# Longformer attention and a softplus MLP in one kernel: queries and keys of the first two batches loaded four tokens to a partition, and the written order of the work made anew

## The chip, the cores and the metric

The kernel runs on one core of a Trainium2 chip. The metric is the device time of one execution in microseconds, the median over the runs; lower is better. The core has a matrix engine (PE, with weight loads PEld), a vector engine (DVE), an activation engine (ACT), a general engine (POOL) and a sync engine (SP) that here only issues transfers. All five run their own written list of instructions in order and wait for one another through semaphores.

## What is computed

Attention over 8 batches, 8 heads, 576 tokens and 64 columns a head: a token sees its neighbours within 32 places, and 8 global tokens see and are seen by all. The result, 4,608 tokens of 512 columns, goes through a two-layer MLP with softplus between.

```python
def _attn_ref(q, k, v, global_idx):
    ...
    scores = scale * np.matmul(q, k.transpose(0, 1, 3, 2))
    mask = np.abs(pos[:, None] - pos[None, :]) <= window      # 32
    mask = mask | is_global[:, None] | is_global[None, :]
    scores = np.where(mask, scores, -1000000000.0)
    scores = scores - np.max(scores, axis=-1, keepdims=True)
    attn = np.exp(scores)
    attn = attn / (np.sum(attn, axis=-1, keepdims=True) + 1e-09)
    return np.matmul(attn, v)

def _moe_ref(x, w_in, w_out):                                 # 512 to 2048 to 512
    h = x @ w_in
    g = np.maximum(h, 0.0) + np.log1p(np.exp(-np.abs(h)))
    return g @ w_out
```

Inputs and output are float32; the products run in bfloat16 with float32 sums.

## The kernel before

**Tiling.** The sequence of a batch is cut into 18 blocks of 32 tokens. Four blocks of all 8 heads make a *pair* (36 pairs over 8 batches, `add_pair`); for a pair, scores of a block against its four key slots (previous, own, next, and one with the global keys) go through mask, maximum `m`, exponential `st`, sum `sm`, reciprocal `rs`, normalisation `pn`, and a 32 by 32 transpose to `pt`. Four pairs make a *phase* of 512 tokens (nine phases). The value products `xo` (L1210) take `pt`, and their result, copied to `xT`, is the input of the MLP: `h` (L1245) with `w_in`, softplus to `g` on ACT (L1251), and `o` (L1256) with `w_out`. The first phase is cut in three pieces (one, two and one pair), the second in two, so that the MLP can start early. Per batch the rows of the global tokens are computed beside that: scores `sg`, maxima `gm`, exponentials `pg`, transposes `pgt`, products `ov`, then `odd`, `both` and `vg`, which the value products need.

**The way in.** Batches 0 and 1 (`b < EARLY`) come in a way of their own: `load_part` loads a part of the sequence of all heads, with `e` neighbouring tokens on one partition, `cast` makes bfloat16 of one `e` of it, `tr` turns it on PE by four transposes and picks the global tokens by four small products (`hot`), and `trev` copies the turned tile from PSUM to `qx` or `kx`, with a stride of `e`. Before, two tokens lie on a partition: a part has 256 tokens, so there are two whole parts and a tail of 64 tokens for q and for k. `FIRST` is the order of the parts. Batches 2 to 7 are loaded by `load_qk` in strips of 32 columns and turned on DVE.

**Queues.** SP issues the loads of q, k and v, in the order of the plan; POOL issues the weights (`w_in` and `w_out`, four pieces each, cast to bfloat16 by the transfer) and most stores. Two things tie the queues together. `follow` lets SP load a few bytes out of `w_in[1]` (or `w_out[1]`), which makes SP wait for that piece before it issues what stands behind (L729). And POOL copies one element of a loaded tile to `seen` before it issues the first weights: of v's first half ahead of `w_in` (L1324), and of a part of batch 1's q ahead of `w_out` (L1388). A load on SP's queue also waits, eight loads later, for the semaphore that it shares with an earlier one.

**The order.** `_Order` is a planner inside the kernel. Every piece of work is a job with costs per engine and dependencies. `ORDER` is a list written out, 1,700 entries and some, that names each next job and its engine (`x // 5`, `x % 5`); a job's planned time `at` sorts them, and each engine's instructions are emitted in that order. So every engine's sequence is fixed by `ORDER`. The planner's costs have an effect on the built program in one place: `keep` puts filler products (`warm`, L706, which compute nothing that is used) on PE where it plans an idle stretch of over 700 ns before 34 us. `stall` models how PE's own instructions are fetched: in blocks of `BLOCK` = 256, the first block asked for at instruction `ASK` = 130 and needed at `NEED` = 442, each taking what `SLOW` says for that time. `settle` shares the transfers between SP's and POOL's queue, `SHARE` = 0.12 for SP when both have work. `SUMMED` names the pairs of the first phase whose sums DVE makes; for the others ACT's exponential adds up as it goes (L1079).

Of the kernel before, what the change touches and what calls it, by code (L numbers as in the profile page):

```python
# [19 lines left out]
class _Order:  # L20
# [20 lines left out]
    SLOW = ((29000, 7000), (37000, 4400), (51000, 6000), (62000, 4200), (150000, 4500), (1e9, 3900))  # L41
# [137 lines left out]
    def run(self, free):  # L179
# [9 lines left out]
        order = []  # L189
# [83 lines left out]
        order.sort(key=lambda j: (j["at"], j["n"]))  # L273
# [9 lines left out]
def kernel(  # L283
# [47 lines left out]
    SUMMED = (2,3,)  # L331
# [169 lines left out]
    for w, t in FIRST[0]:  # L501
        load_part(0, w, t)
# [926 lines left out]
```

## Time and profile before

| | us |
|---|---|
| median of 3 runs | 343.15 |
| lowest and highest | 342.66, 345.87 |
| the profiled execution | 343.51 |
| its span in the trace | 341.8 |
| PE busy | 316.4 |
| DVE busy | 251.3 |
| ACT busy | 221.1 |
| POOL busy | 184.4 |

The span is what the trace records from the first instruction to the last; the time has 1.71 us more around it. Busy time counts an engine's instructions but not its waits. Matmuls are pipelined, so PE's busy time is not its time at full rate, and about one in a hundred of its records is missing, which shows as gaps of 0.16 us. A line with an idle time in brackets says how long the engine had nothing to do just before, and what ended that.

### The profile page before, as it was taken

How to read it: one execution, taken by the hardware profiler on the slowest of the kernel's cores; microseconds unless marked ns; L12 is line 12 of the kernel's file. 1: busy time of each engine (PE TensorE's matmuls, PEld its weight loads, DVE VectorE, ACT ScalarE, POOL GpSimd, SP SyncE). 2: the span in 40 equal slices, each digit the busy share in tenths (PEclk: the TensorE clock that was granted, in tenths of full speed). 3: DMA queues.
4: the chain of work that ended last, by engine and by line, in shares of the span. 5: the costliest groups of instructions: out<-in, count | busy, mean ns of one | idle time of the engine just before them, and what ended most of it. 6: DMA issues, size and time to landing. Idle time of an engine off the chain costs nothing.

```text
span 341.8 us, 12136 instructions
## 1 busy us (share of the span) xinstructions
PE 316.4 (93%) x5278; PEld 171.6 (50%) x5323; DVE 251.3 (74%) x420; ACT 221.1 (65%) x436; POOL 184.4 (54%) x161
## 2 busy tenths in 40 slices
PE   6858889989999999999999999999799989999996
PEld 2725776466555444544554445444344444445453
DVE  7597588987998898999986488979676869631000
ACT  3696768946678868279637775576275747944342
POOL 6474718976696487939548467695415523210000
PEclk9567899999999999999999999999899999999999
DMA  7999399998999899970989798312100111011003
GB/s 192 232 197 256 73 177 169 164 150 169 202 185 175 141 208 199 209 135 31 181 128 181 151 188 224 74 25 46 65 33 11 54 66 63 0 61 63 2 0 123
DMA packets 168733, 42.74 MB, mean 125 GB/s; under 512 B 153192, under 2 KB 165736, under 8 KB 168680
## 3 DMA queue, kind: packets, MB, share of 16 engines
q1 hardware_dynamic: 160664, 28.33, 46.3%
q0 software_dynamic: 6144, 10.49, 13.0%
q10 hardware_dynamic: 1872, 3.15, 2.4%
q8 instruction: 41, 0.67, 0.8%
q14 instruction: 12, 0.10, 0.1%
HBM read 36.71 MB, written 9.44 MB: 135 GB/s over the span
## 4 chain that ended last, share of the span: by engine, by line
PE 66%; DVE 13%; SPq 5%; DMA 5%; issue 4%; ACT 3%; POOL 2%; ACTq 1%; DVEq 0%; POOLq 0%
PE h L1245 28%; PE o L1256 26%; PE xo L1210 4%; SPq L440 3%; PE s L1043 3%; DMA wout<-in_moe_w_out_dram 2%; DVE sm L1090 2%; DMA stage<-in_k_dram 2%; DVE m L1060 2%; SPq L445 2%; DVE st L1047 1%; DVE pt L1107 1%; DVE gm L945 1%; PE ov L968 1%; PE pick L852 1%
## 5 line engine op out<-in xcount | busy, mean ns | idle before, releaser
L1245 PE MATMUL h<-xT,win 128*128 128x512 bf16 (+3 forms) x756 | 136.6, 329 | 1.6 <-DVE xT L698 0.6
L1256 PE MATMUL o<-wout,g 128*128 128x512 bf16 (+1 forms) x561 | 130.9, 375 | 3.8 <-issue 3.2
L1251 ACT ACTIVATE g<-h 128x512 bf16<-128x512 f32 (+3 forms) x192 | 85.4, 496 | 47.9 <-PE h L1245 47.2
L1245 PEld LDWEIGHTS <-win 128*128 128x128 bf16 x768 | 67.3, 99 | 59.6 <-issue 1.3
L1256 PEld LDWEIGHTS <-g 128*128 128x128 bf16 x592 | 55.8, 98 | 63.5 <-issue 2.4
L1098 POOL TENSOR_TENSOR pn<-st,rs 128x1024 bf16<-128x1024 f32 (+1 forms) x36 | 62.4, 1737 | 43.0 <-DVE rs L1092 38.4
L1066 POOL TENSOR_TENSOR st<-st,m 128x1024 f32<-128x1024 f32 x27 | 54.1, 2014 | 48.1 <-DVE m L1060 48.0
L1047 DVE TENSOR_TENSOR st<-s,mask 128x512 f32<-128x512 f32 x64 | 41.3, 678 | 7.1 <-PE s L1043 7.0
L1090 DVE TENSOR_REDUCE sm<-st 128x8 f32<-128x1024 f32 (+1 forms) x36 | 41.1, 1141 | 4.4 <-ACT st L1083 3.8
L1060 DVE TENSOR_REDUCE m<-st 128x8 f32<-128x1024 f32 x32 | 38.1, 1210 | 0.4
L1083 ACT ACTIVATE st<-st 128x1024 f32<-128x1024 f32 x32 | 32.8, 1056 | 1.7 <-POOL st L1066 1.2
L1107 DVE STREAM_TRANSPOSE pt<-pn 128x512 int32<-128x512 int32 x36 | 24.6, 690 | 5.0 <-POOL pn L1098 5.0
L698 ACT COPY osb<-o 128x512 f32<-128x512 f32 (+1 forms) x25 | 14.2, 571 | 18.9 <-PE o L1256 11.8
L698 DVE CAST xT<-xo 128x512 bf16<-128x512 f32 (+3 forms) x25 | 13.1, 567 | 17.4 <-PE xo L1210 17.4
L698 ACT CAST xT<-xo 128x512 bf16<-128x512 f32 (+2 forms) x23 | 9.8, 475 | 19.1 <-PE xo L1210 19.1
L945 DVE TENSOR_REDUCE gm<-sg 128x1 f32<-128x320 f32 (+1 forms) x32 | 12.3, 445 | 9.1 <-PE sg L935 9.1
L1210 PE MATMUL xo<-pt,vb 32*64 32x96 bf16 (+2 forms) x1328 | 14.4, 212 | 4.3 <-issue 4.3
L698 POOL CAST kb<-stage 128x1152 bf16<-128x1152 f32 (+1 forms) x10 | 14.2, 1437 | 7.5 <-DVE st L1047 7.5
L1043 PE MATMUL s<-kx,qx 64*32 64x128 bf16 x1152 | 15.9, 229 | 1.5 <-ACT kx L698 0.7
L1043 PEld LDWEIGHTS <-qx 64*32 64x32 bf16 x1152 | 10.7, 94 | 12.6 <-issue 10.2
L698 POOL CAST vb<-stage 128x1152 bf16<-128x1152 f32 x13 | 15.7, 1223 | 1.6 <-DMA stage<-in_v_dram 1.6
L1210 PEld LDWEIGHTS <-vb 32*64 32x64 bf16 x1328 | 13.8, 104 | 4.9 <-issue 4.6
(125 smaller groups left out, 307.6 us busy)
## 6 DMA issues: line engine op xcount, KB each, us to landing
stage<-in_v_dram SPq DMA_DIRECT2D x64, 144.0 KB, 4.1
stage<-in_k_dram SPq DMA_DIRECT2D x48, 144.0 KB, 3.9
stage<-in_q_dram SPq DMA_DIRECT2D x48, 144.0 KB, 3.9
out_dram<-osb POOLq DMA_DIRECT2D x24, 256.0 KB, 3.4
out_dram<-osb ACTq DMA_DIRECT2D x11, 256.0 KB, 2.0
stage<-in_q_dram SPq DMA_DIRECT2D x4, 512.0 KB, 5.5
stage<-in_k_dram SPq DMA_DIRECT2D x4, 512.0 KB, 8.5
win<-in_moe_w_in_dram POOLq DMA_DIRECT2D x4, 512.0 KB, 7.6
```

Of the source, the lines that this page charges most:

```text
L698: {"ACT": nc.scalar.copy, "DVE": V.tensor_copy, "POOL": nc.gpsimd.tensor_copy}[e](out, in_)
L1043: nc.tensor.matmul(out=PS["s", n, g][quad(a ^ g), x, :], lhsT=qx[b % 2][rows(g), a, j * BL:(j + 1) * BL], rhs=kx[b % 2][rows(g), a, e0 * B ...
L1047: V.tensor_tensor(out=PS["st", n][:, h, :, :], in0=PS["s", n, h][:, :, :], in1=mask[:, h, j0:j0 + PB, :, :].rearrange("p j s i -> p j (s i ...
L1060: V.reduce_max(out=m[:], in_=flat(PS["st", n], h0, h1), axis=AX)
L1066: on(e).tensor_tensor(out=t, in0=t, in1=over(PS["m", n, y][:], SL * BL), op=OP.subtract)
L1083: nc.scalar.activation(out=t, in_=t, func=AF.Exp)
L1090: V.reduce_sum(out=sm[:], in_=flat(PS["st", n], h0, h1), axis=AX)
L1098: on(e).tensor_tensor(out=PS["pn", n][:, :, :, h0:h1].rearrange("p x s h -> p h x s"), in0=PS["st", n][:, h0:h1], in1=PS["rs", n, y][:].re ...
L1210: nc.tensor.matmul(out=PS["xo", v_, hd // 2][hd % 2 * D:(hd % 2 + 1) * D, (x - X0) * BL:(z - X0) * BL], lhsT=lhs, rhs=rhs, start=start, st ...
L1245: nc.tensor.matmul(out=h[:, :], lhsT=w_in_t[c // 4][:, kd, c % 4 * P:(c % 4 + 1) * P], rhs=PS["xT", m][:, kd, lo:hi], start=(kd == 0), sto ...
L1251: nc.scalar.activation(out=PS["g", m, c][:, lo:hi], in_=PS[key][:, lo_of(c, hi - lo)], func=AF.Softplus)
L1256: nc.tensor.matmul(out=PS["o", m, ns, a][:, :], lhsT=PS["g", m, kf][:, ns * P:(ns + 1) * P], rhs=w_out_t[kf // 4][:, kf % 4, a:z], start=( ...
```

## The change

Five things change.

1. For batches 0 and 1 four tokens lie on a partition (`EP = 4`): a part has 512 tokens (1 MB of float32), so there is one whole part and the tail of 64. The casts, transposes and evictions keep their number and sizes; only strides change. The load of q and k of a batch takes 2 transfers of 1 MB, in runs of 1 KB, in place of 4 of 512 KB in runs of 512 B.
2. `FIRST`: k's part comes first, then q's, then the tails. The loads of batch 0 are issued by their jobs, so they too stand where the plan has them: k, q, k's tail, half of v, q's tail, the other half of v.
3. The copy to `seen` ahead of `w_out` reads batch 1's one whole q part, the first of that batch's loads, in place of its second, the last.
4. The planner's numbers: `SLOW` (longer fetches), the lengths of the early loads, the costs of the masked exponentials; `SUMMED` is empty, so ACT adds up in all four pairs of the first phase. Jobs of equal planned time keep the order in which they were planned.
5. `ORDER` is a new list. Every engine's sequence is new: among other things SP issues batch 1's q part ahead of the wait for `w_in[1]`, and the first half of batch 1's v ahead of the wait for `w_out[1]`; the first stretch of `h` has 60 products (48 before) and takes `w_in[3]` after eight of them; two of the eight normalisations of the first phase run on DVE; there are 42 fillers in place of 19, 17 of them at the start, 2, 11, 8 and 4 further on; and the two score blocks of the first two pairs follow each other.

```diff
-    SLOW = ((29000, 7000), (37000, 4400), (51000, 6000), (62000, 4200), (150000, 4500), (1e9, 3900))
+    SLOW = ((30000, 9300), (37000, 6500), (51000, 7300), (62000, 6500), (250000, 5600), (1e9, 4200))
...
-        order.sort(key=lambda j: (j["at"], j["n"]))
+        order.sort(key=lambda j: j["at"])
...
-    SUMMED = (2,3,)
+    SUMMED = ()
...
     ORDER = (
...
-    NTOK = 2 * P
+    EP = 4
+    NTOK = EP * P
     FULL = S // NTOK
-    PARTS = [(t, e) for t in range(FULL) for e in range(2)] + [(FULL, 0)]
+    PARTS = [(t, e) for t in range(FULL) for e in range(EP)] + [(FULL, 0)]
...
-            nc.sync.dma_start(out=flat(stage[w])[:, t * 2 * HD:(t + 1) * 2 * HD].rearrange("p (h x) -> p h x", h=H),
-                              in_=SRC[w][b, :, t * NTOK:(t + 1) * NTOK, :].rearrange("h (p e) d -> p h (e d)", e=2))
+            nc.sync.dma_start(out=flat(stage[w])[:, t * EP * HD:(t + 1) * EP * HD].rearrange("p (h x) -> p h x", h=H),
+                              in_=SRC[w][b, :, t * NTOK:(t + 1) * NTOK, :].rearrange("h (p e) d -> p h (e d)", e=EP))
...
-    FIRST = ([(0, 0), (1, 0), (1, 1), (1, 2), (0, 2), (0, 1)], [(0, 0), (1, 0), (1, 1), (1, 2), (0, 2), (0, 1)])
-    assert FULL == 2
+    FIRST = ([(1, 0), (1, 1), (0, 0), (0, 1)], [(1, 0), (0, 0), (1, 1), (0, 1)])
+    assert FULL == 1
...
-    for w, t in FIRST[0]:
-        load_part(0, w, t)
...
-                if b:
-                    load_part(b, w, t)
+                load_part(b, w, t)
...
-                                       moves=(2000 if b else 1750) if t < FULL else 1500 if b else 600)
+                                       moves=(3500 if b else 3000) if t < FULL else 1300 if b else 650)
...
-                copy(eng, keys[:, :, 4 * t:4 * t + 4, e:2 * BL:2], ps.rearrange("p a (c i) -> p a c i", i=BL))
+                copy(eng, keys[:, :, n * t:n * t + n, e:2 * BL:EP], ps.rearrange("p a (c i) -> p a c i", i=D // EP))
             else:
-                copy(eng, qx[i][:, :, t * NTOK + e:(t + 1) * NTOK:2], ps)
+                copy(eng, qx[i][:, :, t * NTOK + e:(t + 1) * NTOK:EP], ps)
...
-            T["ex", n, y] = o.add({"ACT": act(k, False) if not masked else (720, 820) if n in SUMMED else (1480, 1580)}, lambda e, y=y: ex(e, y), [job, *gate],
+            T["ex", n, y] = o.add({"ACT": act(k, False) if not masked else (1050, 1150) if n in SUMMED else (1390, 1490)}, lambda e, y=y: ex(e, y), [job, *gate],
...
-            T["landed"] = o.add(pool(100), lambda e: nc.gpsimd.tensor_copy(seen[:, 0, :], natural(0, 1)[:, 0, 0, 0, 0:1]), [T["part", 1, 0, FULL]], rank=0)
+            T["landed"] = o.add(pool(100), lambda e: nc.gpsimd.tensor_copy(seen[:, 0, :], natural(0, 0)[:, 0, 0, 0, 0:1]), [T["part", 1, 0, 0]], rank=0)
```

More of the change, by code (lines that the diff above doesn't have):

```diff
@@ L478, in natural @@
         if t < FULL:
-            return x[:, t * 2 * HD:(t + 1) * 2 * HD].rearrange("p (g a e d) -> p g a e d", g=2, a=HG, e=2)
-        return x[:, 2 * FULL * HD:2 * FULL * HD + HD // 2]
+            return x[:, t * EP * HD:(t + 1) * EP * HD].rearrange("p (g a e d) -> p g a e d", g=2, a=HG, e=EP)
+        return x[:, EP * FULL * HD:EP * FULL * HD + HD // 2]
     def rounded(w, t, e):
@@ L484, in rounded @@
         if t < FULL:
-            return x[:, (2 * t + e) * HD:(2 * t + e + 1) * HD]
-        return x[:, 2 * FULL * HD:2 * FULL * HD + HD // 2]
+            return x[:, (EP * t + e) * HD:(EP * t + e + 1) * HD]
+        return x[:, EP * FULL * HD:EP * FULL * HD + HD // 2]
     def load_part(b, w, t):
         if t < FULL:
-            nc.sync.dma_start(out=flat(stage[w])[:, t * 2 * HD:(t + 1) * 2 * HD].rearrange("p (h x) -> p h x", h=H),
-                              in_=SRC[w][b, :, t * NTOK:(t + 1) * NTOK, :].rearrange("h (p e) d -> p h (e d)", e=2))
+            nc.sync.dma_start(out=flat(stage[w])[:, t * EP * HD:(t + 1) * EP * HD].rearrange("p (h x) -> p h x", h=H),
+                              in_=SRC[w][b, :, t * NTOK:(t + 1) * NTOK, :].rearrange("h (p e) d -> p h (e d)", e=EP))
             return
@@ L518 @@
     count(pp[:], [[0, 1]], 0, 1)
-    count(pt_[:, 0:2 * FULL], [[NTOK, FULL], [1, 2]], 0, 2)
+    count(pt_[:, 0:EP * FULL], [[NTOK, FULL], [1, EP]], 0, EP)
     for g in range(2):
-        count(pt_[rows(g), 2 * FULL:], [[0, 1]], FULL * NTOK, 1)
+        count(pt_[rows(g), EP * FULL:], [[0, 1]], FULL * NTOK, 1)
     count(pos[:, P:], [[1, S - P]], P, 0)
@@ L811, in tr @@
         def tr(w, t, e):
-            if e == 0:
-                PS["tr", b, w, t] = psum(("tr", b, w, t), [P, 2, HG, P], BF16)
-            ps = PS["tr", b, w, t]
+            if e % 2 == 0:
+                PS["tr", b, w, t, e // 2] = psum(("tr", b, w, t, e // 2), [P, 2, HG, P], BF16)
+            ps = PS["tr", b, w, t, e // 2]
             own = (qkey, kkey)[w]
@@ L818, in tr @@
             x = rounded(w, t, e)
-            z = 2 * t + e
-            done = [u for v_, u in FIRST[b] if v_ == w][-1] == t and (e or t == FULL)
+            z = EP * t + e
+            done = [u for v_, u in FIRST[b] if v_ == w][-1] == t and (e == EP - 1 or t == FULL)
             for a in range(HG):
                 if t < FULL:
-                    nc.tensor.transpose(out=ps[:, e, a, :], in_=x[:, a * P:(a + 1) * P], identity=ident[:, :])
+                    nc.tensor.transpose(out=ps[:, e % 2, a, :], in_=x[:, a * P:(a + 1) * P], identity=ident[:, :])
                 else:
                     for g in range(2):
-                        nc.tensor.transpose(out=ps[rows(g), e, a, 0:D], in_=x[rows(g), a * D:(a + 1) * D], identity=ident[rows(g), rows(g)])
+                        nc.tensor.transpose(out=ps[rows(g), e % 2, a, 0:D], in_=x[rows(g), a * D:(a + 1) * D], identity=ident[rows(g), rows(g)])
             for a in range(HG):
@@ L836, in trev @@
         def trev(eng, w, t, e):
-            ps = PS["tr", b, w, t][:, e]
+            ps = PS["tr", b, w, t, e // 2][:, e % 2]
+            n = NTOK // D
             keys = near_keys(0, 2 * BL)
             if t == FULL:
-                copy(eng, keys[:, :, 4 * t, :] if w else qx[i][:, :, t * NTOK:], ps[:, :, 0:D])
+                copy(eng, keys[:, :, n * t, :] if w else qx[i][:, :, t * NTOK:], ps[:, :, 0:D])
             elif w:
-                copy(eng, keys[:, :, 4 * t:4 * t + 4, e:2 * BL:2], ps.rearrange("p a (c i) -> p a c i", i=BL))
+                copy(eng, keys[:, :, n * t:n * t + n, e:2 * BL:EP], ps.rearrange("p a (c i) -> p a c i", i=D // EP))
             else:
-                copy(eng, qx[i][:, :, t * NTOK + e:(t + 1) * NTOK:2], ps)
+                copy(eng, qx[i][:, :, t * NTOK + e:(t + 1) * NTOK:EP], ps)
         def pck(e, ws):
@@ L883, in add_prep @@
             for w, t in FIRST[b]:
-                for e in range(2 if t < FULL else 1):
+                for e in range(EP if t < FULL else 1):
                     n = HD if t < FULL else HD // 2
@@ L889, in add_prep @@
                     last = T["last", w]
-                    k_ = ("tr", b, w, t)
+                    k_ = ("tr", b, w, t, e // 2)
                     T["last", w] = T["tr", b, w, t, e] = o.add({"PE": (330, 500) if b else (640, 810) if t == 0 else (500, 670)}, lambda eng, w=w, t=t, e=e: tr(w, t, e),
                                          [job, last, *had("make_ident", "make_hot")], rank=3 if b else 1, ins=16 if t < FULL else 32, array=128 if t < FULL else 64,
-                                         opens=([("tr", k_)] if e == 0 else []) + ([("pick", ("pick", b, w))] if t == e == 0 else []),
-                                         uses=([k_] if e else []) + ([("pick", b, w)] if t + e else []))
+                                         opens=([("tr", k_)] if e % 2 == 0 else []) + ([("pick", ("pick", b, w))] if t == e == 0 else []),
+                                         uses=([k_] if e % 2 else []) + ([("pick", b, w)] if t + e else []))
                     T["cast", b, w].append(job)
```

144 rows, old and new, of the table ORDER are left out of this document.

## The prediction

> **What bounds the kernel now.** I read the page first: busy shares, then the 40 slices.
>
> ```profile
> PE 316.4 (93%) x5278; PEld 171.6 (50%) x5323; DVE 251.3 (74%) x420; ACT 221.1 (65%) x436; POOL 184.4 (54%) x161
> PE   6858889989999999999999999999799989999996
> PEclk9567899999999999999999999999899999999999
> ```
>
> PE is the bound, but for four slices at the front, a dent near slice 28 and the end; its clock is down at the front and in that same dent. PE's products do not change in number, so the time can only change where PE idles or runs at a low clock. The view by stretches shows where (from:to, length, PE busy and, in the first row, the other engines; the last three numbers are clock, DMA share, GB/s).
>
> ```profile
> 36.00:40.00 4.00, 4.00 (x30) 3.05 (x27) 2.81 (x8) 2.18 (x12) 2.37 (x8) 0.57 0.14 38
> 30.00:40.00 10.00, 7.77 (x162) 0.83 0.76 184
> 40.00:50.00 10.00, 8.68 (x253) 1.00 0.82 125
> 50.00:60.00 10.00, 9.53 (x179) 1.00 1.01 176
> 230.00:240.00 10.00, 9.68 (x149) 1.00 0.27 57
> 240.00:250.00 10.00, 7.45 (x242) 0.83 0.17 59
> 250.00:260.00 10.00, 9.95 (x102) 1.00 0.07 25
> ```
>
> Two losses stand out: 30 to 40 us, and 240 to 250. The view of waits for PE and PE's timeline say what they are (start, duration, in brackets the idle time before it).
>
> ```profile
> PE xo L1210 <- issue: 4.3, 2, 2.2
> PE xo L1210 <- DVE pt L1107: 1.6, 2, 1.3
> 29.38 2.84 PE L1245 MATMUL h<-xT,win 128*128 128x128 bf16 x48
> 35.07 0.54 PE L1210 MATMUL xo<-pt,vb 32*64 32x96 bf16 x45 [2.10 <-issue]
> 35.55 4.71 PE L1245 MATMUL h<-xT,win 128*128 128x128 bf16 x34
> 238.53 2.54 PE L1256 MATMUL o<-wout,g 128*128 128x512 bf16 x11 [0.16 <-issue]
> 244.73 0.36 PE L1210 MATMUL xo<-pt,vb 32*64 32x96 bf16 x18 [2.22 <-issue]
> 278.56 0.41 PE L1210 MATMUL xo<-pt,vg 32*64 32x448 bf16 x8 [1.28 <-DVE pt L1107]
> ```
>
> "issue" means that nothing recorded was awaited. I read both as waits for PE's own instructions, because of where they fall. The planner's constants (ASK 130, NEED 442, BLOCK 256) say that a block is asked for 312 instructions, or 156 products with their weight loads, before it is needed. Counted in PE's written order, product 4,317 is a place of need, and PE stopped within two products of it; its block was asked for at product 4,161, the first of the `o` row at 238.5. So that fetch took about 6.2 us (244.7 - 238.5), while the work between took 4.0. The other stop, inside the second `xo` block, is at product 477, again a place of need.
>
> After the first `h` at 29.38 PE has its whole dense work ahead. What the change is worth is when that point comes, and what is idle or slow behind it.
>
> **The opening, part by part.** The rows that carry its chain:
>
> ```profile
> 4.00:6.00 2.00, 2.00 (x7) 0.73 (x6) 1.72 (x7) 0.09 (x1) 1.35 (x4) 1.00 1.16 320
> 7.45 0.62 ACT L698 CAST kb<-stage 128x512 bf16<-128x512 f32 x1 [3.35 <-DMA stage<-in_k_dram]
> 12.41 1.20 POOL L695 TENSOR_SCALAR qb<-stage 128x512 bf16<-128x512 f32 x2 [1.38 <-DMA stage<-in_q_dram]
> 7.63 0.40 DVE L693 TENSOR_SCALAR qb<-stage 128x512 bf16<-128x512 f32 x1
> 10.12 0.74 ACT L698 COPY kx<-tr 128x512 bf16<-128x512 bf16 x1
> 14.71 0.62 PE L1043 MATMUL s<-kx,qx 64*32 64x128 bf16 x30 [0.34 <-ACT kx L698]
> 24.06 1.18 ACT L1075 ACTIVATE st<-s,m 128x128 f32<-128x128 f32 x4
> 24.11 0.29 DVE L959 TENSOR_REDUCE pgt<-own 128x128 bf16<-128x128 bf16 x1
> 25.98 0.63 PE L1043 MATMUL s<-kx,qx 64*32 64x128 bf16 x32
> 26.54 1.46 PE L706 MATMUL warm<-pgt 128*128 128x512 bf16 x3
> 26.57 0.70 DVE L1107 STREAM_TRANSPOSE pt<-pn 128x512 int32<-128x512 int32 x1
> 30.05 1.04 POOL L1098 TENSOR_TENSOR pn<-st,rs 128x512 bf16<-128x512 f32 x1 [0.53 <-DVE rs L1092]
> ```
>
> *Loads.* Before, ACT's first cast at 7.45 had waited for k's first 512 KB, the second such piece, so 1 MB was in by about 7.4. Now k comes first as one 1 MB load: no cast can start before 7.4, but then all four can. q's 1 MB follows: at the 320 GB/s of the first row 3.3 us, so 10.7; by the mean between 7.4 and 12.4 (1.3 MB in 5.0 us, small tails included) 4.0 us, so 11.4. I take 10.7, since tails now stand behind it. Longer runs (1 KB for 512 B) could raise the rate; no row shows one of this kind, and I bound the gain between none and the 0.4 us that 10% of 4 us is. The Trainium skill (DMA: Bandwidth & Descriptors, Specifications) has 512 B as the run from which a transfer goes at full rate; by it the longer runs bring nothing, the value taken here.
>
> *Chain to the first scores.* Three q casts on DVE, 0.40 each, end at 11.9. ACT is held by the cast of k's tail, which lands about 0.5 behind q, until 11.5, and it has the kx and qx evictions queued behind it: five of 0.74, so 15.2. The first score block, 0.62, ends at 15.8; before it ended at 15.33 (14.71 + 0.62). This half us comes back on DVE, which between there and the global maxima has one score maximum and two q evictions of that size fewer; both orders reach the second `pgt` reduction at about 24.4 (24.11 + 0.29).
>
> *Chain to the first h.* Behind that DVE now carries two maxima (0.7 each), the two `odd` copies that ACT had, with their sum and reciprocal (1.0), one normalisation (1.04 by POOL's row) and one transpose (0.70): 28.5. Before, the transpose ended at 27.27. `SUMMED` empty takes four sums from DVE, but later, and adds an accumulator to 16 exponentials of ACT (four took 1.18 without); they lie ahead of the table load, beside the wait for w_in below. Then the value products and xT (1.0 together) and four fillers, 0.9 (0.22 each at full clock) to 1.9 us (1.46 / 3 each); they stand where PE waits for xT, so half is hidden. First `h` at 30.3: **+0.9** against 29.38. Bounds: -0.4 (faster runs, clock held by the 25 fillers between), +2.1 (q at 11.4, fillers at half clock).
>
> *Weights and batch 1.* SP now issues batch 1's first q part (1 MB) ahead of the wait for the second w_in piece. And the first 60 `h` products are in an order that reads the fourth w_in piece after eight products; before, it was read only after the stop at 33. So what the hardware queue takes from w_in's now shows. Rows of the two queues, each over one us (packets, MB, share of 16 engines): from 22, from 4, two from 59 where both ran, and from 29.
>
> ```profile
> q0 software_dynamic: 213, 0.21, 124.6%
> q1 hardware_dynamic: 686, 0.34, 114.8%
> q0 software_dynamic: 153, 0.16, 92.0%
> q1 hardware_dynamic: 152, 0.04, 29.4%
> q0 software_dynamic: 8, 0.01, 4.0%
> ```
>
> Alone, w_in's ended in 29 to 30 us (the last row, the eight packets left there), so it is ready at 30 at best. A 512 B packet costs 1.148 x 16 / 686 = 0.027 us of an engine; a 1 KB one 0.027 to 0.054. 59 to 60 shows packets taken in turn, 153 to 152. The 1,024 packets of that q part then cost w_in 1,024 x 0.027 to 0.054 / 16 = 1.7 to 3.4 us, or nothing where they fall in a gap; the planner's SHARE, 12% for this queue, makes it little. w_in's issue is some 0.7 us earlier, as v's first half now precedes q's tail. Ready at 29.3 to 32.7, needed at 30.8: 0 to 1.9 us, and with a slow clock behind it (1.7, below) 3.6. I take **+1.2**.
>
> *The stop at 33.* The new order has 60 `h` and seven fillers between asking for that block and needing it, 6.5 us of work at full clock against 5.2. It is asked for by about 25, when the chain above is still waiting, and needed after 60 `h` at 34 or later: 9 us. The old fetch took about 8.8 (from the middle of the score block at 25.98 to 35.07). So 2.10 goes, and the slow clock behind it, 0.43 x 4.00 = 1.7 (first row of the stretches): **-3.8**. What is late next is w_in, counted above. The Trainium skill (TensorE: Matmul & The Clock Gate, Part 1) has the clock halve after an idle window of some 3.4 us and return after a busy one; the stop of 2.1 us here was enough to halve it, so the trace decides.
>
> **Behind the opening.** Rows of POOL, which issues the weights, and of SP:
>
> ```profile
> 39.51 0.38 POOL L1388 COPY seen<-stage 128x1 f32<-128x1 f32 x1
> 41.15 1.56 POOL L1311 DMA_DIRECT2D wout<-in_moe_w_out_dram  x2
> 49.88 0.64 SPq L729 DMA_DIRECT2D trail<-wout  x1
> ```
>
> `seen` held back w_out until 41.15, although DMA had been idle since 37 (share 0.14 above). It now waits for the first of batch 1's loads instead of the last, ahead of the last two normalisations; w_out follows them, near 34 to 36. SP's wait at 49.88 for w_out's second piece, with v's other half and all of batch 2 queued behind it, ends as much earlier; v's first half of batch 1 has moved ahead of it. `o` products, which fill PE's gaps, come earlier. Of the 1.32 + 0.47 us idle between 40 and 60 I take back **-0.8** (0 to -1.8).
>
> *The stop at 244.* In the new order each span of 156 products around there carries 6.0 us or more, where 4.4 stood (0.22 us for 512 columns, 0.059 for 128, 0.011 for score and value products). Both losses, 2.22 and 0.17 x 10 = 1.7, go: **-3.9**. But some spans stay short: 4.8 (unchanged, near 285 us, no stop before), 5.2, 5.4, 5.8. Old spans of 4.4 to 5.2 elsewhere passed without one, so most fetches are quicker than the one of 6.2: **+1.0** for new stops (0 to 3.9, one like the old).
>
> *All else in the sequence.* Every engine's order is new. Before, PE waited for `pt` 1.6 us in all; waits of that kind may go or come: **+0.5** (-1.3 to +4).
>
> Sum: 0.9 + 1.2 - 3.8 - 0.8 - 3.9 + 1.0 + 0.5 = -4.9. The profiled execution took 343.51 us (span 341.8, 1.71 around it): 338.6. It lies 0.36 above the median of 343.15, which I leave alone.
>
> **Rivals.**
>
> *w_in is late.* q's part and half of batch 1's k (1.5 x 3.4 us at the dear price) go packet for packet with w_in; the fourth piece lands near 34, PE stops for three us after eight `h`, and its clock halves again. The term +1.2 becomes +4.7: 342.1. For it: 59 to 60 above. The Trainium skill (DMA: Bandwidth & Descriptors, Queues, rings and completion order) says that an engine takes its queues in turn by packets; by that rule this rival comes about, and the trace agrees in that one us. Against it: part of q's load may run before w_in starts.
>
> *The fetch stops move instead of going.* If 6 to 7 us are usual, the spans of 4.8 to 5.8 stop PE; two of them with slow clock give back 2 x 3.9 - 1.0: 345.4; one gives 341.5. Against it: the old order had nine such spans with no stop above 0.4 us.
>
> *Slower: the new order asks too early for `pt`.* PE keeps its written order, so an `xo` block ahead of its transpose stops everything behind. The row at 278.56 is such a wait, 1.28 us. One of 2.2 us would also halve the clock, as at 244, and cost 3.9. Two of these over seven batches give 338.6 - 0.5 + 7.8 = 345.9, three 349.8; from three it is slower by over 1%. For it: DVE is busy 74% and gets normalisations. Against it: no block but that one waited over 0.6 us, and the dense products on both sides are the same.
>
> *The change does nothing:* not possible for the loads; the time would be 343.
>
> **How the numbers follow.** Forecast 0.5; w_in late 0.17; fetch stops moved 0.15; slower order 0.18. One per cent, 3.4 us, is what a measurement here can tell from none. Below 339.7 lies the forecast (its bad edge is balanced by the others' good ones): faster 0.50. Within: the two middle rivals, 0.32. Over 346.6: 0.18. The forecast's own range is 334.5 (the good ends of first h, w_out and new stops, -1.3 - 1.0 - 1.0, and most of w_in's 1.2) to 340.5; for 8 in 10 it must reach the middle rivals, to 345.5.
>
> **What would show it.** First `h` at 30 to 31 and full clock from there; no "issue" wait of 2 us in an `xo` row near 35 or 240; w_out issued before 37; PE idle in 240 to 250 below 0.5. Wrong would be: PE idle after the first eight `h`; first `h` behind 32; PE's waits for `pt` over 4 us in all; an "issue" wait of 2 us elsewhere.

## The result, and the profile after

The changed kernel is slower: 353.22 us median of 4 runs (352.16 to 354.03), against 343.30 for the kernel before on the same chip. The ratio is 1.031, with an interval of 1.026 to 1.035. The forecast was 338.6, with a range that ended at 345.5. Here and below, runs over 1.5% above the fastest of their kernel stay in the medians and are left out of the ratios.

The profiled execution took 353.58 us; its page, with PE's busy time first, then PE's busy share and granted clock in 40 slices:

```profile
span 351.6 us, 12227 instructions
PE 326.0 (93%) x5346; PEld 171.9 (49%) x5346; DVE 262.5 (75%) x417; ACT 230.7 (66%) x458; POOL 173.2 (49%) x154
PE   7486788999999799899999999799999999999996
PEclk9769899999999999999999999699999999999999
```

The clock's dent has moved from slice 28, counted from 0, to slice 25 (220 to 229 us), and PE is thinner than before in slices 1, 3, 4 and 6, and in 13 and 16. PE's waits (us in all, times, the longest) and its timeline (start, duration, in brackets the idle time before) name the losses:

```profile
PE xo L1209 <- issue: 4.7, 2, 2.8
PE h L1244 <- DMA win<-in_moe_w_in_dram: 3.1, 1, 3.1
PE s L1042 <- ACT qx L697: 3.1, 2, 1.6
PE o L1255 <- issue: 1.2, 1, 1.2
```

```profile
17.18 0.63 PE L1042 MATMUL s<-kx,qx 64*32 64x128 bf16 x32 [1.45 <-ACT qx L697]
32.75 0.22 PE L1244 MATMUL h<-xT,win 128*128 128x128 bf16 x1
33.58 0.55 PE L1244 MATMUL h<-xT,win 128*128 128x128 bf16 x7 [0.62 <-DVE xT L697]
37.25 2.96 PE L1244 MATMUL h<-xT,win 128*128 128x128 bf16 x27 [3.12 <-DMA win<-in_moe_w_in_dram]
53.71 0.91 PE L1042 MATMUL s<-kx,qx 64*32 64x128 bf16 x32 [1.65 <-ACT qx L697]
116.11 0.33 PE L1209 MATMUL xo<-pt,vb 32*64 32x96 bf16 x27 [1.92 <-issue]
145.81 1.45 PE L1255 MATMUL o<-wout,g 128*128 128x512 bf16 x6 [1.22 <-issue]
221.83 0.66 PE L1209 MATMUL xo<-pt,vb 32*64 32x96 bf16 x47 [2.78 <-issue]
```

The first scores come at 17.18 (14.71 before, behind two products at 14.09), the first `h` at 32.75 (29.38 before), and after eight of the 60 `h` products PE stops 3.12 us for `w_in[3]`. Both old stops for "issue", near 35 and 244, are gone. Three others have come, at 116, 146 and 222 us (slices 13, 16 and 25), and the clock is low behind the longest, as it is behind the stop for `w_in[3]`. The view by stretches shows that (length, PE busy, the other engines, then clock, DMA share, GB/s):

```profile
30.00:40.00 10.00, 5.63 (x120) 4.46 (x120) 7.47 (x16) 7.36 (x37) 6.51 (x8) 0.83 1.06 210
220.00:230.00 10.00, 8.17 (x132) 3.74 (x132) 6.33 (x10) 4.10 (x6) 2.13 (x4) 0.66 0.83 183
```

What held the first scores back stands on ACT, in the group of evictions (L697 of after, the `copy` helper). The first fence is ACT's timeline, the second the view of groups over the first 60 us, for after (count | busy, mean ns of one); the third is the same view for before.

```profile
10.78 0.41 ACT L697 CAST kb<-stage 128x256 bf16<-128x256 f32 x1 [2.14 <-DMA stage<-in_k_dram]
11.09 1.35 ACT L697 COPY kx<-tr 128x512 bf16<-128x512 bf16 x1
12.16 1.41 ACT L697 COPY qx<-tr 128x512 bf16<-128x512 bf16 x1
13.31 1.39 ACT L697 COPY kx<-tr 128x512 bf16<-128x512 bf16 x1
14.45 2.68 ACT L697 COPY qx<-tr 128x512 bf16<-128x512 bf16 x2
```

```profile
L697 ACT COPY qx<-tr 128x512 bf16<-128x512 bf16 x4 | 5.5, 1371 | 0.0
L697 DVE COPY qx<-tr 128x512 bf16<-128x512 bf16 x4 | 5.1, 1272 | 0.1
```

```profile
L698 ACT COPY qx<-tr 128x512 bf16<-128x512 bf16 x5 | 3.6, 772 | 0.5 <-PE tr L823 0.5
L698 DVE COPY qx<-tr 128x512 bf16<-128x512 bf16 x3 | 2.1, 720 | 0.0
```

The instructions have the same shape and the same types in both kernels. They differ in one thing that no column shows: before, a copy writes every second bfloat16 of `qx` or `kx` (2 bytes in every 4), and now every fourth (2 bytes in every 8). That takes 1.27 to 1.37 us in place of 0.72 to 0.77. ACT's five stand in a row from 11.09 to 17.13 (their records overlap, and one starts every 1.1 us or so), and the score block at 17.18 waits for the last.

### The profile page after: what moved, and what is told of

It reads as the page before. It is cut to its first block, busy times and chain, and to the rows that moved or that the text cites. A ratio compares the mean times of both kernels' runs of the same rounds, so it can differ in the third digit from the quotient of the medians.

```text
span 351.6 us, 12227 instructions
## 1 busy us (share of the span) xinstructions
PE 326.0 (93%) x5346; PEld 171.9 (49%) x5346; DVE 262.5 (75%) x417; ACT 230.7 (66%) x458; POOL 173.2 (49%) x154
## 4 chain that ended last, share of the span: by engine, by line
PE 74%; SPq 6%; DMA 5%; DVE 5%; ACT 3%; issue 3%; POOL 2%; POOLq 0%; ACTq 0%
PE o L1255 32%; PE h L1244 31%; SPq L440 5%; PE xo L1209 4%; DMA stage<-in_k_dram 3%; PE s L1042 3%; DMA win<-in_moe_w_in_dram 3%; ACT kx L697 1%; PE ov L967 1%; PE pick L851 1%; POOL pn L1097 1%; ACT qx L697 1%; PE sg L934 1%; POOL qb L694 1%; DVE qx L697 1%
## 5 line engine op out<-in xcount | busy, mean ns | idle before, releaser
L1255 PE MATMUL o<-wout,g 128*128 128x512 bf16 (+1 forms) x592 | 137.7, 376 | 1.2 <-issue 1.2
L1250 ACT ACTIVATE g<-h 128x512 bf16<-128x512 f32 (+3 forms) x192 | 86.6, 503 | 51.0 <-PE h L1244 50.4
L1244 PEld LDWEIGHTS <-win 128*128 128x128 bf16 x768 | 68.6, 100 | 64.8 <-issue 4.2
L1065 POOL TENSOR_TENSOR st<-st,m 128x1024 f32<-128x1024 f32 x27 | 52.8, 1967 | 53.2 <-DVE m L1059 53.0
L1097 POOL TENSOR_TENSOR pn<-st,rs 128x1024 bf16<-128x1024 f32 (+1 forms) x32 | 55.9, 1758 | 43.2 <-DVE rs L1091 35.0
L1089 DVE TENSOR_REDUCE sm<-st 128x8 f32<-128x1024 f32 x32 | 38.2, 1194 | 4.5 <-ACT st L1082 4.5
L697 DVE CAST xT<-xo 128x512 bf16<-128x512 f32 (+3 forms) x23 | 12.3, 566 | 20.5 <-PE xo L1209 20.4
L697 ACT CAST xT<-xo 128x512 bf16<-128x512 f32 (+3 forms) x25 | 10.8, 485 | 25.1 <-PE xo L1209 22.4
L697 ACT COPY osb<-o 128x512 f32<-128x512 f32 (+1 forms) x26 | 14.9, 572 | 16.2 <-PE o L1255 13.7
L1267 POOL DMA_DIRECT2D out_dram<-osb x24 | 13.9, 581 | 15.6 <-DVE osb L697 10.8
L697 POOL CAST kb<-stage 128x1152 bf16<-128x1152 f32 (+1 forms) x11 | 14.6, 1349 | 10.0 <-DVE m L1059 9.5
L1209 PEld LDWEIGHTS <-vb 32*64 32x64 bf16 x1328 | 13.7, 103 | 5.4 <-issue 4.9
```

The lines of the kernel that those rows point to most:

```text
L697: {"ACT": nc.scalar.copy, "DVE": V.tensor_copy, "POOL": nc.gpsimd.tensor_copy}[e](out, in_)
L1065: on(e).tensor_tensor(out=t, in0=t, in1=over(PS["m", n, y][:], SL * BL), op=OP.subtract)
L1089: V.reduce_sum(out=sm[:], in_=flat(PS["st", n], h0, h1), axis=AX)
L1097: on(e).tensor_tensor(out=PS["pn", n][:, :, :, h0:h1].rearrange("p x s h -> p h x s"), in0=PS["st", n][:, h0:h1], in1=PS["rs", n, y][:].re ...
L1209: nc.tensor.matmul(out=PS["xo", v_, hd // 2][hd % 2 * D:(hd % 2 + 1) * D, (x - X0) * BL:(z - X0) * BL], lhsT=lhs, rhs=rhs, start=start, st ...
L1244: nc.tensor.matmul(out=h[:, :], lhsT=w_in_t[c // 4][:, kd, c % 4 * P:(c % 4 + 1) * P], rhs=PS["xT", m][:, kd, lo:hi], start=(kd == 0), sto ...
```

## The experiments

The theory was that these copies cost most of the loss, through the opening, and that fetch stops at new places cost the rest; the rivals were the order around `w_in[3]` and the transfers. All runs, with the median of the kernel before on the same chip (343.72 for e1 to e4, 342.95 for e5 to e7, 343.75 for e8, 344.70 for e9), and from the traces the span, the first `h` and batch 1's first `ov` row:

| | median us (runs) | ratio, interval | span | first h | ov, batch 1 |
|---|---|---|---|---|---|
| before | 343.30 | – | 341.8 | 29.38 | 68.53 |
| after | 353.22 (4) | 1.031, 1.026 to 1.035 | 351.6 | 32.75 | 73.21 |
| e1, contiguous | 347.12 (8) | 1.005, 0.999 to 1.012 | 345.3 | 31.34 | 68.74 |
| e2, every second | 346.30 (1) | – | 344.3 | 31.19 | 65.67 |
| e3, w_in[3] early | 350.58 (2) | 1.019, 1.010 to 1.028 | 348.3 | 33.18 | 69.78 |
| e4, e1 and e3 | 345.80 (8) | 0.993, 0.986 to 1.000 | 343.5 | 30.10 | 64.62 |
| e5, pairs and e3 | 346.41 (12) | 1.010, 1.007 to 1.014 | 342.4 | 31.28 | 66.02 |
| e6, before, every fourth | 349.39 (4) | 1.019, 1.014 to 1.024 | 347.9 | 32.39 | 74.84 |
| e7, 64 more products | 364.48 (2) | 1.063, 1.055 to 1.072 | 365.3 | 32.74 | 77.23 |
| e8, before, pairs | 340.67 (7) | 0.992, 0.990 to 0.994 | 342.2 | 29.01 | 67.72 |
| e9, no late loads | 350.07 (2) | 1.017, 1.000 to 1.034 | 349.7 | 33.29 | 71.96 |

Kernel e4's eight runs spread from 339.4 to 352.6 and its ratio rests on three of them; I read it as no difference from before. Kernel e2 ran once, so it has no interval.

**The step of the writes alone: e1, e2.** In e1 each copy writes its 512 elements side by side, in runs of 128, in e2 in every second place; tokens of batches 0 and 1 then stand in another order, and nothing else is changed. The line for `qx` is shown, e1's and then e2's; that for `kx` is alike, here and below.

```diff
-                copy(eng, qx[i][:, :, t * NTOK + e:(t + 1) * NTOK:EP], ps)
+                copy(eng, qx[i][:, :, t * NTOK + e * P:t * NTOK + (e + 1) * P], ps)
...
-                copy(eng, qx[i][:, :, t * NTOK + e:(t + 1) * NTOK:EP], ps)
+                copy(eng, qx[i][:, :, t * NTOK + e // 2 * 2 * P + e % 2:t * NTOK + (e // 2 + 1) * 2 * P:2], ps)
```

> The changed kernel, but the copies of the turned tiles of batches 0 and 1 write their 512 elements side by side instead of every fourth place, so tokens of these batches stand in another order in qx and kx. Same instructions, same order. Theory 1 (writing every fourth bf16 place is what made these copies 1.3 us long): they take 0.75 us again, the first score block starts at 15 to 16 instead of 17.2, the first h at 31 to 32 instead of 33.6, and the time falls by 3 to 5 us to 348 to 350, since batch 1 gains too. Theory 2 (the length has to do with more work side by side on ACT and DVE, not with the stride): copies stay at 1.2 us or more and the time within 1 us of 353. Theory 3 (the new written order and the late fourth piece of w_in set the time): copies get short, but PE still starts its fifth group of h at 36 or later and the time falls by less than 1.5 us.

> As the run before, but the copies write every second place, as the kernel before did (tokens of batches 0 and 1 again in another order). If a write of every second place is free and one of every fourth is not, the copies take 0.75 us and the time is that of the side-by-side copies within 0.7 us. If the price grows with the distance, they take about 1.0 us and the time lies halfway.

The groups of copies in e1, then in e2, and two rows of PE's timeline in e2:

```profile
L697 ACT COPY qx<-tr 128x512 bf16<-128x512 bf16 x4 | 2.4, 594 | 0.2 <-PE tr L821 0.2
L697 DVE COPY qx<-tr 128x512 bf16<-128x512 bf16 x4 | 1.6, 394 | 0.1
```

```profile
L697 ACT COPY qx<-tr 128x512 bf16<-128x512 bf16 x4 | 3.0, 741 | 0.5 <-DVE qx L697 0.3 <-PE tr L821 0.2
L697 DVE COPY qx<-tr 128x512 bf16<-128x512 bf16 x4 | 2.8, 709 | 0.1
```

```profile
15.17 0.63 PE L1042 MATMUL s<-kx,qx 64*32 64x128 bf16 x32
32.49 3.08 PE L1244 MATMUL h<-xT,win 128*128 128x128 bf16 x52 [0.21 <-DMA win<-in_moe_w_in_dram]
```

Kernels e2 and after have the same order on PE, so times at one place can be compared directly: batch 1's first `ov` row comes 7.5 us sooner (65.67 against 73.21) and the end 7.3 sooner (344.3 against 351.6). The step of the writes is thus worth some 7 us, all of it in the opening. The runs say the same, with a wide spread: e2's one run is 6.9 us under the median of after, and the median of e1's eight 6.1 (they lie between 342.7 and 350.4), where theory 1 had 3 to 5. Going on to contiguous writes makes the copies shorter again (0.39 to 0.59 against 0.71 to 0.74) but brings no more time, 347.1 against 346.3: the first scores come at 15.12, as in e2, and wait for a copy in neither; and e1 has two more waits for "issue" in the opening, 1.1 and 1.35 us. The stop for `w_in[3]` all but goes as well, so it was in good part a consequence of the late copies.

**w_in[3] alone: e3, e4.** The reason stands in POOL's timeline of after:

```profile
25.86 2.04 POOL L1097 TENSOR_TENSOR pn<-st,rs 128x512 bf16<-128x512 f32 x2 [5.91 <-DVE rs L1091]
27.84 0.81 POOL L1306 DMA_DIRECT2D win<-in_moe_w_in_dram  x1
38.20 1.56 POOL L1310 DMA_DIRECT2D wout<-in_moe_w_out_dram  x2
```

The issue of the last `w_in` piece stands behind two normalisations, and these wait for DVE until 25.86. One entry of `ORDER` was moved, 68 to right behind 63, so that POOL issues this piece together with the third: in e3 in the changed kernel, in e4 together with e1's edit.

> The changed kernel with one job moved in the written order: POOL issues the fourth piece of w_in right behind the third, ahead of the cast of v and of two normalisations. Theory 1 (POOL's place in line made it late): it is issued near 18 instead of 27.8, lands by 32, PE does not wait for it (3.1 us less idle, some of the half-speed stretch from 37 to 40 goes too), time 349 to 350.5. Theory 2 (batch 1's q load, taken in turn with it, made it late): it still lands after 35 and the time stays within 1 us of 353.

> Both edits of the first and third run at once (tokens of batches 0 and 1 in another order). If the two costs are of different things they add: first h at 31 to 32 and no wait behind it, time 345 to 347. If both act through the same wait, it is no better than the better of the two, 348 to 350. What is then left against the kernel before (343.3) would be the stops of PE on its own instructions at 116, 146 and 222.

In e3 the issue is at 16.49 and the stop is gone: one row of 59 `h` products runs from 34.01 on. The span is 3.3 us shorter. With e1's edit it brings less, 1.8 us in the spans of e4 and e1, which is well inside the spread of their runs, and in e4 PE still waits 1.0 us there, as it arrives earlier. The late issue is thus what made the stop in the changed kernel. The loads, which my rival had blamed, had a part in it all the same: in after, from 28 to 32 us, `w_in`'s queue moved 57 packets while that of the loads moved 1,139; and in e5 below, which has the early issue too, PE still waits 1.46 us for the piece, until 33.88, after a stretch (24 to 28 us) in which 372 packets of the loads went between 561 of the weights. What the loads alone would have cost was not measured.

**The other way round: e6.** The kernel before with every fourth place written, in stretches of 256 tokens, whose tokens then stand in another order.

```diff
-                copy(eng, qx[i][:, :, t * NTOK + e:(t + 1) * NTOK:2], ps)
+                copy(eng, qx[i][:, :, t * NTOK:(t + 1) * NTOK].rearrange("p a (i h e) -> p a h i e", h=2, e=2)[:, :, :, :, e], ps.rearrange("p a (h i) -> p a h i", h=2))
```

> The kernel before, with only its evictions changed: within each stretch of 256 tokens of batches 0 and 1 the 512-element copy writes every fourth place (8 bytes apart) in place of every second; the tokens of a stretch stand in another order, so scores are of other pairs; nothing else differs. Theory (the 8-byte step is the main loss of the changed kernel): the copies go from 0.73 to about 1.3 us, the first score block comes 1.3 to 2.5 us later than 14.71, and the kernel becomes 3 to 7 us slower, 346 to 350. Rival (the loss is of the loading and the sequence, the copies are hidden): within 1.5 us of before, 342 to 345.

The groups, and a row of PE's timeline:

```profile
L698 ACT COPY qx<-tr 128x512 bf16<-128x512 bf16 x5 | 6.5, 1357 | 1.0 <-PE tr L823 1.0
L698 DVE COPY qx<-tr 128x512 bf16<-128x512 bf16 x3 | 3.7, 1306 | 0.0
```

```profile
16.88 0.62 PE L1043 MATMUL s<-kx,qx 64*32 64x128 bf16 x30 [1.38 <-ACT kx L698]
```

The theory held: the copies take 1.31 to 1.36, the score block comes 2.2 us later (16.88 against 14.71), and the kernel is 1.9% slower. Batch 1's `ov` row is 6.3 us later and the span 6.1 longer. The one edit that the description of the change calls a change of strides thus costs the kernel before nearly what it costs the changed one, 6.1 us of span against 7.3.

**Fewer, wider writes: e5, e8.** One copy of 1024 elements evicts two tokens of a partition, which lie side by side: 4 bytes in every 8 in the changed kernel (e5, with e3's move), all bytes in the kernel before (e8). Every token stands where it did. The edit of e8 is shown; e5's does the same for each of its two pairs.

```diff
-            ps = PS["tr", b, w, t][:, e]
+            if t < FULL and e == 0:
+                return
+            pair = PS["tr", b, w, t]
...
-                copy(eng, qx[i][:, :, t * NTOK + e:(t + 1) * NTOK:2], ps)
+                copy(eng, qx[i][:, :, t * NTOK:(t + 1) * NTOK].rearrange("p a (i e) -> p a i e", e=2), pair.rearrange("p e a i -> p a i e"))
```

> The changed kernel with the evictions of batches 0 and 1 in pairs: one copy of 1024 elements writes tokens 4p and 4p+1 (then 4p+2 and 4p+3) side by side, so 4 bytes every 8 bytes, in place of two copies of 512 that write 2 bytes every 8; every token stands where it did. w_in[3] is issued early as in e3_win3_early. Theory (the copy pays for the memory that its writes span, 4 KB for 512 elements in the changed kernel): a pair costs what one single copy costs now, 1.3 to 1.5 us on DVE and on ACT, so half the copy time goes; time near e4_contig_win3's 345.8 and e2_stride2's 346.3, 343 to 348. Rival (it pays 2.5 ns for each element wherever it goes): a pair costs 2.5 to 2.7 us and the time stays at e3_win3_early's 350 to 351.

> The kernel before with its evictions of batches 0 and 1 in pairs: one copy of 1024 elements for both tokens of a partition, which then lie side by side, in place of two copies of 512 that each write every second place; nothing else, every token stands where it did. Theory (the path of the opening runs through these copies in the kernel before too, at 0.73 each): a pair costs 0.9 to 1.2 us against 1.45 for two, the first score block and batch 1's come 0.3 to 1 us sooner, and the time is 341 to 343, 0 to 2 us under before. Rival (what e2_stride2 and e5_pair_win3 gained is special to the changed kernel's order; here the first half now waits for the second's transposes): no change or up to 2 us slower, 343 to 345.

The groups of copies in e5, then in e8, and two rows of PE's timeline in e8:

```profile
L697 ACT COPY qx<-tr 128x1024 bf16<-128x1024 bf16 x2 | 1.9, 1030 | 0.0
L697 DVE COPY qx<-tr 128x1024 bf16<-128x1024 bf16 x2 | 2.4, 1222 | 0.1
```

```profile
L698 ACT COPY qx<-tr 128x1024 bf16<-128x1024 bf16 x3 | 3.1, 1019 | 1.2 <-PE tr L823 1.2
L698 DVE COPY qx<-tr 128x1024 bf16<-128x1024 bf16 x1 | 1.2, 1215 | 0.0
```

```profile
13.95 0.94 PE L1047 MATMUL s<-kx,qx 64*32 64x128 bf16 x32
29.01 2.84 PE L1249 MATMUL h<-xT,win 128*128 128x128 bf16 x48 [0.22 <-ACT xT L698]
```

A pair costs 1.01 to 1.22 with gaps behind it or without, less than one single copy of half the elements in the changed kernel. So the idea that a copy pays for the memory its writes span, from which e5's 1.3 to 1.5 came, is not what happens: e5 spreads its writes over twice the memory of e8 at the same price. In e8 the first score block ends 0.4 us sooner (13.95 + 0.94 against 14.71 + 0.62), batch 1's `ov` comes 0.8 sooner (67.72 against 68.53), and e8 is faster than both kernels: 0.992 of before, interval 0.990 to 0.994, 3.1 us where 0 to 2 were expected. Its profiled execution was the slowest of its seven, 343.96, so the spans do not show the gain; the runs do.

**The count of products: e7.** Of the first 17 fillers of 512 columns six stay and the rest become 75 of 8 columns, so that everything behind stands 64 products later in PE's count.

```diff
-        for x in range(n):
+        first_fill.append(key)
+        cols = [512] * n if len(first_fill) > 1 else [512] * 6 + [8] * (n - 6 + 64)
+        for c in cols:
...
```

> The changed kernel with 64 more TensorE products at its very start (11 of the 17 first fillers of 512 columns become 75 of 8 columns, which take no longer), nothing else. Theory (the waits put down to issue are fetches of TensorE's own instructions, which fall at every 128th product counted from the program's start): the stops leave products 2013, 2525 and 3805 and come at what were products 1437, 2077, 3357, 3869, 4381 and 4893 (about 87, 119, 189, 224, 259 and 292 us), where the next 156 products take only 1.7 to 3.2 us: five or six stops of 2 to 5 us, in all 12 to 30 us more, 364 to 384. Rival (the waits for issue come of busy transfers at those times, not of a count): the stops stay at 116, 146 and 222 us and the time stays within 2 us of 353.

PE's timeline, all rows that waited over 0.5 us for "issue" from 60 us on:

```profile
122.28 0.62 PE L1046 MATMUL s<-kx,qx 64*32 64x128 bf16 x29 [2.15 <-issue]
195.00 0.35 PE L1046 MATMUL s<-kx,qx 64*32 64x128 bf16 x22 [2.21 <-issue]
229.72 0.61 PE L1046 MATMUL s<-kx,qx 64*32 64x128 bf16 x50 [2.14 <-issue]
266.63 0.29 PE L1046 MATMUL s<-kx,qx 64*32 64x128 bf16 x11 [2.35 <-issue]
301.42 0.20 PE L1213 MATMUL xo<-pt,vb 32*64 32x32 bf16 x2 [2.63 <-issue]
```

The three stops of after are gone, and these five stand where the count puts them: behind the places 28, 20, 47 and 8 products of the score blocks should be left in the first four rows, and 29, 22, 50 and 11 are; the fifth is three products early too. The sixth place that was named, near 87 us, shows 0.43 only. The kernel is 11 us slower than after, at the lower edge of what was expected. Of the 13.7 us between the spans the stops make 5.6 (five of 11.5 in all for three of 5.9); 4.0 are there already at batch 1's `ov` (77.23 against 73.21), and the rest is not assigned. That the waits for "issue" are fetches of PE's own instructions at counted places is thus shown. The Trainium skill (Runtime: NRT & Kernel Launch, Instruction fetch mechanics) has instructions come in blocks of 256 and calls the cost of a boundary mostly hidden; the blocks agree with these places, the second half does not, where the 156 products ahead of a place take less than a fetch.

**How long a fetch takes: e9.** The view of transfers has the fetches as a queue of their own, queue q8, one packet of 16 KB each. In the eleven traces every stop for "issue" of over 0.9 us ends 2.2 to 3.1 us after such a packet starts, so what varies is when the packet starts. For the stop that ended at 221.83 the ask is by the count at 212.9, but the packet appears only in the second of these windows of after, 213 to 219 and 219 to 220.5 us (packets, MB, share of 16 engines):

```profile
q1 hardware_dynamic: 6544, 0.85, 89.2%
...
q8 instruction: 1, 0.02, 4.1%
```

So the block lies 6 us unfetched while the loads of q and v (queue q1) run; by the same count more than half of this kernel's 42 packets start within 2 us of the ask. In e9 the loads of q, k and v for batches 3 to 7 are left out, and the engines work on what batch 2 left.

```diff
-                    load_v(nc.sync, b, h, range(R))
+                    if b < 3:
+                        load_v(nc.sync, b, h, range(R))
...
-            T["load", b, w] = o.add({"DMA": (4400, 0)}, lambda e: load_qk(nc.sync, b, w, (0, 2, 1, 3)), deps, rank=0,
+            T["load", b, w] = o.add({"DMA": (4400, 0)}, lambda e: load_qk(nc.sync, b, w, (0, 2, 1, 3) if b < 3 else ()), deps, rank=0,
```

> The changed kernel without the loads of q, k and v for batches 3 to 7 (the engines then work on what batch 2 left, and all products, stores and weights stay). What it tells: in the changed kernel the packet of the block that PE waits for at 222 us starts only at 219.4, 6.4 us after the ask by my count, where 0.7 to 1.5 us is usual. Theory (the packet is late because the hardware queue of those loads keeps the transfer engines busy): the three stops at products 2013, 2525 and 3805 (116, 146 and 222 us, 5.9 us of waiting) go or fall under 1 us in all, with the slow clock behind the last, and the kernel ends 6 to 9 us sooner, span 343 to 346. Rival (the place in the count alone decides, whatever else the transfer engines do): all three stay within 0.7 us of their length, span 350 to 352.

PE's timeline at the three places:

```profile
113.84 0.32 PE L1210 MATMUL xo<-pt,vb 32*64 32x96 bf16 x27 [0.93 <-issue]
143.35 4.26 PE L1256 MATMUL o<-wout,g 128*128 128x512 bf16 x19 [1.59 <-ACT st L1083]
218.00 0.56 PE L1210 MATMUL xo<-pt,vb 32*64 32x96 bf16 x47 [1.66 <-issue]
```

Neither side won (span 349.7, where 343 to 346 or 350 to 352 was expected). The first and the last stop are 1.0 and 1.1 us shorter (0.93 for 1.92, 1.66 for 2.78). In the middle the profile puts the wait down to ACT; a packet started 3.0 us before its end, so it may be the old stop still. By the count the packets of the first and the last still start over 4 and over 5 us behind the ask, with no load in the way. The busy transfers make about one microsecond of these two. What makes the rest is open.

## Why the prediction was wrong

The profiled execution came 15.0 us above the forecast (353.58 against 338.6). Kernel e2 is the change with the copies at the price I had assumed, and it took 346.3. So the price of the copies is 7.3 of the 15.0, and other terms are 7.7. This rests on e2's one run; with the median of e1 it would be 6.5.

1. *The chain to the first scores* is the step that failed first: "five of 0.74, so 15.2". The row of 0.74 was of a copy that writes every second place; the instruction to be priced writes every fourth. I took over the statement that only strides change as if a stride had no price. ACT was free at 11.19 (10.78 + 0.41), near the 11.5 forecast, so the loads were right; the five copies, of 1.35 to 1.41, then took from 11.09 to 17.13, 6.0 us for the 3.7 of the sum. In e2 the first score block ends at 15.80 (15.17 + 0.63), where the sum has 15.8, though it no longer waits for a copy there. No bound of mine held this case, as the bounds were of the loads and of the fillers. The trace of before has no such copy with a wider step, so this was an unknown cost, to be bounded from both sides, and not an edit with one answer. The Trainium skill (Advanced Engine Details and Errata, Memory Cachelines) has accesses to SBUF at full performance as long as each line of 16 bytes is hit twice; at a step of 8 bytes it is. The trace differs: 1.36 against 0.74 at a step of 4 and 0.59 without one, on ACT.
2. *The first h, +0.9*, came at +3.37; with the cheap copies of e2 at +1.81, inside my bounds of -0.4 to +2.1.
3. *w_in, +1.2 at most 3.6*: PE stopped as in the rival that I gave 0.17, after eight `h`, for 3.12 us, with a slow clock behind it. My reason for the rival was only half right: the loads did go ahead of the piece, but first of all it was issued late, at 27.84, because POOL's two `pn` ahead of it waited for DVE (e3). I had counted what stands ahead of `w_out` on POOL's queue but not what stands ahead of `w_in[3]`.
4. *The old stops, -3.8 and -3.9*: both are gone. Near 244 there are 6.0 us of work ahead of the place where 4.0 stood, as forecast, though its packet also came sooner (1.1 us after the counted ask, for 3.6 before). Near 33 there is luck in it. I had the block asked for by about 25; by the count it was asked for at 28.8 in after and 27.7 in e2, and in after PE stood for `w_in` before it needed it. In e1, where the stop for `w_in` is down to 0.21, PE waits 1.09 us for "issue" in the same `xo` block, at 37.07.
5. *New fetch stops, +1.0* is the second step that failed, and the larger part of the 7.7. In e2 they are 1.38, 1.38 and 2.53 us, with a clock of 0.83 over ten microseconds around the last (1.7 lost): 7.0 in all. From PE's timeline and the view by stretches of e2:

```profile
108.33 0.33 PE L1209 MATMUL xo<-pt,vb 32*64 32x96 bf16 x27 [1.38 <-issue]
137.64 2.53 PE L1255 MATMUL o<-wout,g 128*128 128x512 bf16 x11 [1.38 <-issue]
213.37 0.66 PE L1209 MATMUL xo<-pt,vb 32*64 32x96 bf16 x47 [2.53 <-issue]
```

```profile
212.00:222.00 10.00, 8.63 (x140) 4.20 (x140) 6.78 (x10) 5.34 (x8) 2.37 (x4) 0.83 0.92 201
```

   From short spans that had passed I inferred that most fetches are quick and sorted the new spans by their work alone: 4.8 to 5.8 in danger, 6.0 and over safe. The stops fell in spans of 5.8 and 6.2, and the one of 4.8 passed again. In e1 to e5, whose order on PE is that of after, stops of 1.0 to 3.1 us stand at these three places every time. The places were predictable, the length of a fetch was not. The rival that the stops move, with 345.4 for two, is the one whose mechanism came about.
6. *w_out, -0.8*: issued at 38.20, not at 34 to 36; earlier than before by 3 us.
7. *All else, +0.5*: after has no wait of PE for `pt` over 0.7 us from 60 us on; the rival that needed three of them, the only one on the slow side, did not come about. e2 has one of 2.34, at 248.43 (before had 1.6 in all), and its clock stays at 1.00 from 240 to 260: one such wait need not cost the 3.9 of that rival.

With the measured sizes in the place of the assumed ones, e2 comes to 338.6 + 0.9 (first `h`, 1.81 for 0.9) - 1.0 (w_in, 0.2 for 1.2) + 6.0 (stops, 7.0 for 1.0) = 344.5; the other 1.8 us of its 346.3 are not assigned.

The order's own share is seen behind the opening. From batch 1's first `ov` row to the end, before took 273.3 us (341.8 - 68.53) and e6 273.1; after took 278.4 and e2 278.6. By row rates the products left there differ by only 0.8 us between the two orders. So the new order loses some 4 us behind the opening whatever the copies cost, and its fetch stops are the larger part of that (7.0 us in e2 against 2.22 and 1.7 before). That is why e5, which reaches batch 1's `ov` 2.5 us sooner than before (66.02 against 68.53), has no shorter span, though its profiled execution was the fastest of its twelve.

## What to carry to other kernels

A copy's price is read from a row with the same step of its writes, not from one with the same shape and type: the profile's columns do not show the step, so where a change alters a stride, look it up in the code and treat the cost as unknown until a run has it. Where neighbouring elements end up side by side, one copy that writes both is cheaper than two that leave gaps; here that alone made the tuned kernel 0.8% faster. And before a stop of PE is counted as gone, count its instructions in the new order: every 128th product is a place where it can stop, and a safe span there must be longer than the longest fetch seen, not than a usual one.

## What the runs showed of the hardware

The time of an eviction from PSUM, by what it writes, as means of groups of equal copies (first DVE, then ACT): 512 bfloat16 side by side 0.39 to 0.42 and 0.59 us; 2 bytes of every 4, 0.71 to 0.72 and 0.73 to 0.77; 2 bytes of every 8, 1.27 to 1.31 and 1.32 to 1.38. A copy of 1024 in pairs took 1.22 and 1.01 to 1.03, whether 4 bytes of every 8 were written or all of them. The mechanism behind this was not tested further.

A stop of PE for its own instructions ended 4.0 to 4.5 us after the counted ask at the five places of e7, and 6.7 to 9.0 us after it at the three of the changed kernel. Around the stop of 2.78 us that ended at 221.83 the clock was at 0.66 from 220 to 230. A shorter stop had that effect only at times: of the five in e7, 2.14 to 2.63 us long, three left it at 1.00 over ten microseconds (193 to 203, 228 to 238, 265 to 275), while behind those that ended at 122.28 and 301.42 it was at 0.83 (120 to 130, 300 to 310).
